# Starting every SBUF tile of a TensorE-bound kernel at a multiple of 128 bytes

## The chip, the cores and the metric

The kernel runs on one core of one Trainium2 chip. The metric is the device time of one execution in microseconds (us). The names of the engines are those of the profile: PE is TensorE's matmul, PEld its weight load, DVE VectorE, ACT ScalarE, POOL GpSimd, SP SyncE, whose queue issues the transfers.

## What is computed

Three parts follow each other: a recurrent attention over 768 steps (32 heads in 4 batches, head size 48), a dense gated layer, and a dense mixture of eight experts whose gates are normalised eight times over rows and columns. Cut to what matters:

```
state = zeros(B, H, D, D)                         # B, H, S, D = 4, 8, 768, 48
for t in range(S):
    cur = einsum('bhd,bhe->bhde', u * k[t], v[t])
    y[t] = einsum('bhd,bhde->bhe', r[t], state + cur)
    state = w[t][..., None] * state + einsum('bhd,bhe->bhde', k[t], v[t])
x = y as (3072, 384)
x = ((x @ w1) * (x @ w2) @ w3) @ w_out            # inner width 1024
P = exp(x @ w_gate - max), 8 times scaled by its row sums and column sums
out = sum over e in 0..7 of P[:, e] * (relu(x @ w1[e]) @ w2[e])   # 384 -> 1024 -> 384
```

## The kernel before

**Split products.** The matmuls that carry the weight are float32r ones (four bytes an element, in one pass). A float32 operand is split into a high part and a low part, and a product is the sum of three matmuls: high by high, and the two mixed ones. So each such product is three matmuls into one PSUM bank. A few smaller products (`w34ps`, `trn`, `sc`, `yt`, `up`, `pl`) are plain float32 ones.

**Attention and dense part** (up to some 440 us). The attention goes in 24 units of 128 steps. Its steps are written out by hand in the table `START` and then in slices of the main loop; the dense layer's matmuls `pa`, `pb` (inputs by `w1h`, `w1l`, `w2h`, `w2l`) and `po` (`w34h`, `w34l` by `gh`, `gl`) fill the same order, 576 of each, every one with 384 moving columns. The product of the third and the output weights, `w34ps`, is made at the start by plain float32 matmuls of 384 columns.

**Experts** (the rest). `phase(n)`, n from 0 to 63, is one pair of weight blocks (k = n // 4) with one quarter of the tokens (sb = n % 4). The first layer is a matrix product with 15 instead of 18 block products: each of the 15 products is six matmuls `zp`, of 256 columns, with the stationary operand from `w1c` and the moving one from `xc`. VectorE and ScalarE put the products together in `ct` and split the result in `hh` (high) and `hl` (low). The second layer runs one phase behind: matmuls `yp` with `hh` or `hl` stationary and the weights `w2h`, `w2l` moving, 384 columns. Between two products of `zp` stand three, six or nine `yp`; the order of the program decides, since all of it is written in order and nothing is scheduled at run time. The weights of block i lie in the tiles `w1c` number i % 3 and `w2h`/`w2l` number i % 4; phases of block pair k use the first-layer weights 2k and 2k+1.

**Where tiles lie.** Tile pools are stacked from the left of a partition's SBUF (const, moe, mw, att, later m2) or from its right (tmp, later wp, m1, xp). Every tile takes its size in bytes a partition, rounded up to 32. A few tiles of odd size (`d1`, `lowb`, `nat_w`, `Ft`, `Gt`, `T12`, `cc`, and in the experts' part `mx`, `nmx`, `rs`, `cs`) shift all that follow them on their side, and the right side's upper end is not at a multiple of 128 either. In the built program, the tiles that matmuls of the heavy kind read start here (bytes in a partition, and the rest on division by 128):

```
tile                          before: start, rest      after: start, rest
w1h, w1l, w2h, w2l (dense)    89440.., 96              89600.., 0
w34h, w34l, gh, gl, xhl       20320.., 96              20480.., 0
xc0, xc1, xc2, xc3            149472.., 96             149376.., 0
w1c number 0 and 1            145376.., 96             145280.., 0
w1c number 2                  71456.., 32              71936.., 0
w2h, w2l number 0 and 1       126944.., 96             126848.., 0
w2h, w2l number 2 and 3       55072.., 32              55552.., 0
hh, hl                        22304.., 32              22784.., 0
wo, w3c (plain float32)       44896.., 96              45056.., 0
```

Inside these tiles a matmul's operand starts a multiple of 512 bytes on, so that the rest of the tile's start is also that of the operand. A stationary operand is 512 bytes of each partition, a moving one 1024 (`zp`) or 1536 bytes.

Of the kernel before, what the change touches and what calls it, by code (L numbers as in the profile page):

```python
# [11 lines left out]
F32 = mybir.dt.float32  # L12
F32R = mybir.dt.float32r
BF16 = mybir.dt.bfloat16
# [47 lines left out]
def tile_rwkv_moe_sinkhorn_moe(  # L62
# [19 lines left out]
    B, H, S, D = SHAPE  # L82
    NT, DM = out.shape
    P = 128
    FF = moe_w3.shape[0] * P
    E = e_w2.shape[0] * 2 * P // FF
    DP = 64
    NP = H // 2
# [7 lines left out]
    NTT = NT // P  # L96
# [19 lines left out]
    const = ctx.enter_context(tc.tile_pool(name="const", bufs=1))  # L116
    ident = const.tile([P, P], F32, name="ident")
    mask = const.tile([P, DP], F32, name="mask")
    eye = const.tile([P, DP], F32, name="eye")
    d1 = const.tile([P, 16 * 33 + 1], BF16, name="d1")  # L120
    GP = 32
    gate = const.tile([P, KD, GP], F32, name="gate")
    lowb = const.tile([P, 1], F32, name="lowb")
    nc.vector.memset(lowb, LOW_BIAS)
    lt = const.tile([GP * UB, P], F32, name="lt")
    nc.vector.memset(gate, 0.0)
# [9 lines left out]
    for c in range(2):  # L136
        nc.scalar.activation(eye[64 * c:64 * c + 64, :], ident[64 * c:64 * c + 64, 64 * c:64 * c + 64], AF.Copy)
        nc.gpsimd.affine_select(out=mask[64 * c:64 * c + 64, :], in_=mask[64 * c:64 * c + 64, :],
                                compare_op=ALU.is_gt, fill=0.0, base=0, pattern=[[1, DP]],
                                channel_multiplier=-1)  # L140

    st_moe = ExitStack()
    moe = st_moe.enter_context(tc.tile_pool(name="moe", bufs=1))
# [3 lines left out]
    att = st_attn.enter_context(tc.tile_pool(name="att", bufs=1))  # L147
# [8 lines left out]
    SRC = {"r": (rt, NP * P), "k": (kt, NP * P), "v": (v, H * DP), "w": (w, 16 * 33 + 1),  # L156
           "rn": (rn, H * D), "kn": (kn, H * D)}
    nat = {}
    for nm in SRC:
        for j in range(2):  # L160
            nat[nm, j] = att.tile([P, SRC[nm][1]], F32, name=f"nat_{nm}{j}")

    def load(u_, nms):
        for nm in nms:
# [96 lines left out]
    st = defaultdict(dict)  # L261
# [7 lines left out]
    def tot(n):  # L269
        return st[n]["F"].rearrange("p (b s) -> p b s", s=33).rearrange("p (c b) s -> p b c s", b=2)  # L270
# [4 lines left out]
        nc.gpsimd.tensor_tensor(t, t, ub, op=ALU.mult)  # L275

    def scan_f(n):
        st[n]["F"] = t = att.tile([P, 528], F32, tag="F", name="Ft")
        nc.vector.tensor_tensor_scan(t, nat["w", n % 2][:, 0:528], d1[:, 0:528], 0.0, op0=ALU.mult, op1=ALU.add)

    def scan_g(n):
        st[n]["G"] = t = att.tile([P, 529], F32, tag="G", name="Gt")
        nc.vector.tensor_tensor_scan(t[:, 2:529][:, ::-1], nat["w", n % 2][:, 2:529][:, ::-1],
                                     d1[:, 2:529][:, ::-1], 0.0, op0=ALU.mult, op1=ALU.add)

    def small(n):
        d, tv = st[n], tot(n)[:, :, :, 32]
        d["M"] = att.tile([P, 2, 8], F32, tag="M", bufs=2, name="Mt")
        d["T12"] = att.tile([P, NP, 2], F32, tag="T12", bufs=2, name="T12")
        nc.vector.reciprocal(d["M"], tv)  # L290
        nc.vector.tensor_tensor(d["T12"].rearrange("p a b -> p (a b)"), tv[:, 0, :], tv[:, 1, :], op=ALU.mult)

# [20 lines left out]
                                    op=ALU.mult)  # L313

    def cc(n):
        st[n]["cc"] = t = att.tile([P, H], F32, tag="cc", bufs=2, name="cc")
        nc.vector.tensor_reduce(t, st[n]["rk"], axis=AX.X, op=ALU.add)

    def ec(n):
# [104 lines left out]
    def stage_a0(n):  # L424
        rk(n)
        aux.extend([lambda f=f: f(n) for f in (scan_f, scan_g, small, ks, rp, kx, rx)] + [lambda: (cc(n), ec(n))])
# [345 lines left out]
    def ld_u():  # L772
        nc.sync.dma_start(ub.rearrange("p h d -> p (h d)"), u.rearrange("h d -> (h d)").partition_broadcast(P))

    STEP = dict(ld=ld, lw=lw, ex=ex_, jn=jn, hi=hi, lo=lo, w34=w34, ws=ws, w34l=w34l_, ldu=ld_u, rk=rk, scanF=scan_f, scanG=scan_g,
                small=small, ks=ks, rp=rp, kx=kx, rx=rx, cc=cc, ec=ec, sc=sc, trn=trn, kn=kn_, cp=cp_, yt1=yt1, up=up_,
                Sn=sn_, yt2=yt2, xraw=xraw, xd=xd_, xh=x_high, xl=x_low, pa=pa, asb=asb, pb=pb, gs=gs, gh=gh_, gl=gl_,
                po=moe_x2, L=lambda nm, n: load(n, (nm,)))
# [5 lines left out]
    for s in range(S0, NSL):  # L784
        n, ph = s // 4, s % 4
# [60 lines left out]
    so = {}  # L846

    def open2():
        st_ps.close()
        st_moe.close()  # L850
        m2 = pools["m2"] = ctx.enter_context(tc.tile_pool(name="m2", bufs=1, reuse_waits="tile"))
        pools["y"] = ctx.enter_context(tc.tile_pool(name="ps2", bufs=1, space=PSUM, reuse_waits="tile"))
        for nm, sh in (("ones", [P, P]), ("Pm", [P, NTT, E]), ("mx", [P, 1]), ("nmx", [P, 1]), ("mrow", [1, P]),
                       ("rs", [P, NTT]), ("cs", [P, E])):
            so[nm] = m2.tile(sh, F32, name=nm)
        nc.vector.memset(so["ones"], 1.0)

    hb = {}
# [64 lines left out]
    def phase(n):  # L923
# [8 lines left out]
        def after(r):  # L932
            if ORDER.index(r) % 4 == 3 or r == ORDER[-1]:
                release(n, GOF[r])
            while at["slot"] in due:
                for f in due.pop(at["slot"]):
                    f()
            at["slot"] += 1
            if ex:
                ex.popleft()()  # L940
            if sk and at["sk"] and ORDER.index(r) in SKP:
                sk.popleft()()
            if n == 0:
                i_ = ORDER.index(r)
                if i_ < PO:
                    moe_x2(NB - 1, i_, PO)
                if i_ == PO - 1:
                    open2()
                if i_ == 11:
                    y_fill(0)  # L950
                y_units((0, 0, 2, 2, 4)[max(0, i_ - 10)])
            elif n == 1:
                y_units(YN1[r])
            else:
                y_units(YN[r])
# [283 lines left out]
```

## Time and profile before

| what | value |
|---|---|
| three timed runs, us | 1945.58, 1946.57, 1946.62 |
| median, us | 1946.57 |
| profiled execution, us | 1946.4, from first to last instruction; no other time of it is shown |
| granted TensorE clock | 1.000 of full speed in every stretch shown |
| busy: PE, PEld | 1919.9 us (99%), 1872.1 us (96%) |
| busy: DVE, ACT, POOL | 1381.8 us (71%), 686.2 us (35%), 647.2 us (33%) |

Busy time of matmuls comes from modelled ends and overlaps: a matmul of 337 ns can follow the one before after half that time. What one matmul costs in a row of them is the step from one to the next, which the chain of work that ended last shows as a piece's length over its count.

### The profile page before, as it was taken

How to read it: one execution, taken by the hardware profiler on the slowest of the kernel's cores; microseconds unless marked ns; L12 is line 12 of the kernel's file. 1: busy time of each engine (PE TensorE's matmuls, PEld its weight loads, DVE VectorE, ACT ScalarE, POOL GpSimd, SP SyncE). 2: the span in 40 equal slices, each digit the busy share in tenths (PEclk: the TensorE clock that was granted, in tenths of full speed). 3: DMA queues.
4: the chain of work that ended last, by engine and by line, in shares of the span. 5: the costliest groups of instructions: out<-in, count | busy, mean ns of one | idle time of the engine just before them, and what ended most of it. 6: DMA issues, size and time to landing. Idle time of an engine off the chain costs nothing.

```text
span 1946.4 us, 38115 instructions
## 1 busy us (share of the span) xinstructions
PE 1919.9 (99%) x15499; PEld 1872.1 (96%) x15499; DVE 1381.8 (71%) x2409; ACT 686.2 (35%) x1322; POOL 647.2 (33%) x867
## 2 busy tenths in 40 slices
PE   6999999999999999999999999999999999999999
PEld 3799999999999999999999999999999999999999
DVE  7865777765887876666767676666676767667666
ACT  6733333344333333233333233333333333333322
POOL 6856666635332312222222222221313231312200
PEclk9999999999999999999999999999999999999999
DMA  9632444347655555454545555555454555555453
GB/s 371 228 95 81 138 132 137 104 151 247 224 177 202 184 190 187 174 213 172 202 177 193 186 193 181 187 185 195 172 202 176 199 188 186 188 179 189 167 202 118
DMA packets 90494, 353.76 MB, mean 182 GB/s; under 512 B 10384, under 2 KB 34256, under 8 KB 64592
## 3 DMA queue, kind: packets, MB, share of 16 engines
q1 hardware_dynamic: 90320, 351.34, 51.4%
q8 instruction: 122, 2.00, 0.4%
q14 instruction: 52, 0.43, 0.1%
HBM read 329.67 MB, written 20.45 MB: 180 GB/s over the span
## 4 chain that ended last, share of the span: by engine, by line
PE 96%; DVE 2%; DMA 1%; ACT 1%; issue 0%; SPq 0%; DVEq 0%; ACTq 0%
PE yp L114 41%; PE zp L114 35%; PE po L114 5%; PE pa L114 5%; PE pb L114 4%; PE w34ps L114 2%; PE yt L114 1%; PE sc L114 1%; PE trn L114 1%; PE up L114 1%; DMA raw<-in_moe_w_out_dram 0%; PE pl L114 0%; DMA raw<-in_moe_w_dram 0%; DVE cvp L229 0%; DMA xraw<-xraw 0%
## 5 line engine op out<-in xcount | busy, mean ns | idle before, releaser
L114 PE MATMUL zp<-xc,w1c 128*128 128x256 f32 x5760 | 815.4, 281 | 1.0 <-DVE ct L894 0.5
L114 PEld LDWEIGHTS zp<-xc,w1c 128*128 128x128 f32 x5760 | 783.6, 189 | 3.8 <-DVE ct L897 1.4
L114 PE MATMUL yp<-w2h,hh 128*128 128x384 f32 x1536 | 516.9, 337 | 0.0
L114 PE MATMUL yp<-w2h,hl 128*128 128x384 f32 x1536 | 516.3, 336 | 0.5 <-DVE hl L891 0.5
L114 PE MATMUL yp<-w2l,hh 128*128 128x384 f32 x1536 | 513.9, 335 | 0.0
L886 ACT ACTIVATE hh<-ct 128x512 fp32r<-128x512 f32 x384 | 237.1, 632 | 538.1 <-DVE ct L894 269.8
L894 DVE TENSOR_TENSOR ct<-ct,zp 128x512 f32<-128x512 f32 x576 | 381.0, 683 | 53.2 <-PE zp L114 47.5
L616 POOL TENSOR_TENSOR w1c<-w1s,w1c 128x512 fp32r<-128x512 f32 (+1 forms) x120 | 127.7, 1064 | 796.4 <-PE yp L114 487.9
L901 ACT ACTIVATE ct<-zp 128x512 f32<-128x512 f32 x256 | 153.3, 599 | 455.9 <-PE zp L114 455.9
L114 PEld LDWEIGHTS yp<-w2h,hh 128*128 128x128 f32 x1536 | 290.9, 189 | 0.2 <-issue 0.2
L114 PEld LDWEIGHTS yp<-w2h,hl 128*128 128x128 f32 x1536 | 288.1, 188 | 1.0 <-DVE hl L891 0.9
L114 PEld LDWEIGHTS yp<-w2l,hh 128*128 128x128 f32 x1536 | 288.3, 188 | 0.0
L1066 DVE SCALAR_TENSOR_TENSOR acc<-yp,Pm,acc 128x384 f32<-128x384 f32 x336 | 205.5, 612 | 109.4 <-PE yp L114 109.2
L891 DVE SCALAR_TENSOR_TENSOR hl<-ct,hh 128x512 fp32r<-128x512 f32 x384 | 273.8, 726 | 0.0
L897 DVE TENSOR_TENSOR ct<-ct,zp 128x512 f32<-128x512 f32 x128 | 88.0, 688 | 168.4 <-PE zp L114 168.4
L897 DVE TENSOR_TENSOR ct<-zp,ct 128x512 f32<-128x512 f32 x128 | 88.3, 690 | 78.2 <-PE zp L114 69.6
L616 POOL TENSOR_TENSOR w1c<-w1raw,w1c 128x128 fp32r<-128x128 f32 (+1 forms) x90 | 55.0, 612 | 205.6 <-ACT w1c L612 205.6
L608 POOL TENSOR_TENSOR w1s<-w1raw 128x128 f32<-128x128 f32 x240 | 121.0, 525 | 0.2
L483 POOL TENSOR_TENSOR gl<-gs,gh 128x384 fp32r<-128x384 f32 x64 | 74.2, 1160 | 109.3 <-ACT gh L479 106.6
L114 PE MATMUL pa<-xhl,w1h 128*128 128x384 f32 x384 | 101.7, 345 | 1.2 <-ACT w34s L255 1.2
L114 PE MATMUL pb<-xhl,w2h 128*128 128x384 f32 x384 | 98.1, 336 | 0.4 <-DVE cv L230 0.4
L474 DVE TENSOR_TENSOR gs<-pb,asb 128x384 f32<-128x384 f32 x64 | 35.4, 553 | 71.5 <-PE pb L114 49.3
(130 smaller groups left out, 1906.2 us busy)
## 6 DMA issues: line engine op xcount, KB each, us to landing
xc<-xd SPq DMA_DIRECT2D x192, 1024.0 KB, 4.8
xc<-xd SPq DMA_DIRECT2D x64, 768.0 KB, 4.3
xd<-x2s SPq DMA_DIRECT2D x53, 256.0 KB, 2.8
w1raw<-in_e_w_dram SPq DMA_DIRECT2D x32, 384.0 KB, 3.1
w2raw<-in_e_w_dram SPq DMA_DIRECT2D x32, 384.0 KB, 3.1
raw<-in_moe_w_dram SPq DMA_DIRECT2D x8, 1024.0 KB, 8.9
nat_w<-in_w_dram SPq DMA_DIRECT2D x24, 264.5 KB, 3.3
nat_k<-in_kt_dram SPq DMA_DIRECT2D x24, 256.0 KB, 4.0
```

The lines of the kernel that those rows point to most:

```text
L114: nc.tensor.matmul(o, lhsT, rhs, start=start, stop=stop, **kw)
L474: nc.vector.tensor_tensor(t, m_t.pop(("pb", blk, f)), m_t.pop(("asb", blk, f)), op=ALU.mult)
L483: nc.gpsimd.tensor_tensor(gl[:, f, :], m_t.pop(("gs", blk, f)), gh[:, f, :].bitcast(F32), op=ALU.subtract)
L608: eng.tensor_tensor(tmp_[:, many.index(r), :], at_(a), at_(b), op=ALU.add if sg == 1 else ALU.subtract)
L616: eng.tensor_tensor(lo[:, d0:d1, :], sv, hi[:, d0:d1, :].bitcast(F32), op=ALU.subtract)
L886: nc.scalar.activation(hh, src, AF.Relu)
L891: nc.vector.scalar_tensor_tensor(hl, src, 0.0, hh.bitcast(F32), op0=ALU.max, op1=ALU.subtract)
L894: nc.vector.tensor_tensor(o, a, b_, op=ALU.add)
L897: nc.vector.tensor_tensor(o, a, b_, op=ALU.subtract)
L901: nc.scalar.activation(t, src, AF.Copy)
L1066: nc.vector.scalar_tensor_tensor(dst, yp, so["Pm"][:, tt, e:e + 1], dst, op0=ALU.mult, op1=ALU.add)
```

## The change

A tile of 96 bytes that nothing reads is put at the right end (`edge`), and the tiles of odd size are allocated with more elements and cut back to the old shape by a slice, so that each operand has the same shape as before. With that nearly every tile begins at a multiple of 128 bytes (the tiles `Mt`, `T12` and `cc` of 64 bytes come in pairs, and the second of a pair begins 64 bytes on). No instruction is added, removed or moved: on each engine the program has the same instructions in the same order with the same waits. The tile `mrow` of m2 now stands ahead of the four small ones.

```diff
-    d1 = const.tile([P, 16 * 33 + 1], BF16, name="d1")
+    d1 = const.tile([P, 16 * 36], BF16, name="d1")[:, 0:16 * 33 + 1]
     GP = 32
     gate = const.tile([P, KD, GP], F32, name="gate")
-    lowb = const.tile([P, 1], F32, name="lowb")
+    lowb = const.tile([P, GP], F32, name="lowb")[:, 0:1]
...
+    edge = ctx.enter_context(tc.tile_pool(name="edge", bufs=1, side="right"))
+    edge.tile([P, 24], F32, name="edge")
...
-            nat[nm, j] = att.tile([P, SRC[nm][1]], F32, name=f"nat_{nm}{j}")
+            nat[nm, j] = att.tile([P, -(-SRC[nm][1] // 32) * 32], F32, name=f"nat_{nm}{j}")[:, 0:SRC[nm][1]]
...
-        st[n]["F"] = t = att.tile([P, 528], F32, tag="F", name="Ft")
+        st[n]["F"] = t = att.tile([P, 544], F32, tag="F", name="Ft")[:, 0:528]
...
-        st[n]["G"] = t = att.tile([P, 529], F32, tag="G", name="Gt")
+        st[n]["G"] = t = att.tile([P, 544], F32, tag="G", name="Gt")[:, 0:529]
...
-        d["T12"] = att.tile([P, NP, 2], F32, tag="T12", bufs=2, name="T12")
+        d["T12"] = att.tile([P, 2 * NP, 2], F32, tag="T12", bufs=2, name="T12")[:, 0:NP, :]
...
-        st[n]["cc"] = t = att.tile([P, H], F32, tag="cc", bufs=2, name="cc")
+        st[n]["cc"] = t = att.tile([P, 2 * H], F32, tag="cc", bufs=2, name="cc")[:, 0:H]
...
-        for nm, sh in (("ones", [P, P]), ("Pm", [P, NTT, E]), ("mx", [P, 1]), ("nmx", [P, 1]), ("mrow", [1, P]),
-                       ("rs", [P, NTT]), ("cs", [P, E])):
+        for nm, sh in (("ones", [P, P]), ("Pm", [P, NTT, E]), ("mrow", [1, P])):
             so[nm] = m2.tile(sh, F32, name=nm)
+        for nm, n_ in (("mx", 1), ("nmx", 1), ("rs", NTT), ("cs", E)):
+            so[nm] = m2.tile([P, 32], F32, name=nm)[:, 0:n_]
```

## Rows read from the trace of the kernel before

**Rows 1.** Cores: span and mean granted TensorE clock.

```profile
core 0: 1946.4 us, clock 1.000
```

**Rows 2.** The page: busy time of each engine, share, instructions.

```profile
PE 1919.9 (99%) x15499; PEld 1872.1 (96%) x15499; DVE 1381.8 (71%) x2409; ACT 686.2 (35%) x1322; POOL 647.2 (33%) x867
```

**Rows 3.** Chain that ended last: shares by engine (page), by line (chain view).

```profile
PE 96%; DVE 2%; DMA 1%; ACT 1%; issue 0%; SPq 0%; DVEq 0%; ACTq 0%
...
by line: PE yp L114 41.0%; PE zp L114 34.8%; PE po L114 5.3%; PE pa L114 4.8%; PE pb L114 4.5%; PE w34ps L114 1.8%; PE yt L114 1.3%; PE sc L114 0.6%; PE trn L114 0.6%; PE up L114 0.5%; DMA raw<-in_moe_w_out_dram 0.5%; issue 0.4%; PE pl L114
```

**Rows 4.** Groups of PE by line and shape: count, busy, mean ns.

```profile
L114 PE MATMUL zp<-xc,w1c 128*128 128x256 f32 x5760 | 815.4, 281 | 1.0 <-DVE ct L894 0.5 <-DVE ct L897 0.5
L114 PE MATMUL yp<-w2h,hh 128*128 128x384 f32 x1536 | 516.9, 337 | 0.0
L114 PE MATMUL w34ps<-wo,w3c 128*128 128x384 f32 x128 | 47.2, 521 | 3.2 <-DVE w3c L230 3.2
```

**Rows 5.** Chain in order of time, early stretch: start us, us, what.

```profile
34.15 0.44 PE trn L114 x4
49.70 8.39 PE w34ps L114 x26
```

**Rows 6.** The same chain: dense part, experts, and the last piece.

```profile
128.12 3.12 PE po L114 x18
1013.51 1.43 PE zp L114 x12
1929.37 13.54 PE yp L114 x78
```

**Rows 7.** Stretches of four phases, k = 6 to 13: busy by engine, clock, DMA.

```profile
1004.06:1097.18 93.12, 93.12 (x649) 93.03 (x649) 64.63 (x103) 30.49 (x58) 23.13 (x38) 1.00 0.53 187
1097.18:1189.50 92.32, 92.32 (x649) 92.23 (x649) 64.32 (x103) 30.22 (x57) 23.11 (x38) 1.00 0.54 188
1189.50:1281.73 92.23, 92.23 (x649) 92.12 (x649) 64.37 (x103) 30.30 (x57) 23.22 (x38) 1.00 0.54 189
1281.73:1374.59 92.86, 92.86 (x650) 92.77 (x649) 64.55 (x103) 30.44 (x58) 23.20 (x38) 1.00 0.53 187
1374.59:1467.41 92.82, 92.82 (x649) 92.74 (x649) 64.41 (x103) 30.36 (x58) 23.16 (x38) 1.00 0.52 188
1467.41:1559.73 92.32, 92.32 (x650) 92.23 (x649) 64.32 (x103) 30.27 (x58) 23.14 (x38) 1.00 0.53 188
1559.73:1652.85 93.12, 93.12 (x650) 93.03 (x649) 64.62 (x103) 30.50 (x58) 23.13 (x38) 1.00 0.53 187
1652.85:1745.17 92.32, 92.32 (x650) 92.23 (x649) 64.32 (x103) 30.23 (x57) 23.11 (x38) 1.00 0.54 188
```

**Rows 8.** Stretches of 20 us after the experts begin: same columns.

```profile
480.00:500.00 20.00, 19.75 (x140) 19.17 (x140) 16.79 (x31) 9.13 (x17) 9.92 (x17) 1.00 0.90 308
580.00:600.00 20.00, 20.00 (x141) 19.90 (x140) 17.93 (x35) 8.23 (x16) 5.65 (x9) 1.00 0.59 211
```

**Rows 9.** Who waited for whom, PE: total us, times, longest.

```profile
PE sc L114 <- POOL Rt L312: 14.0, 1, 14.0
PE w34ps L114 <- DVE w3c L230: 3.2, 2, 2.6
```

**Rows 10.** Who waited for whom, all engines: total us, times, longest.

```profile
ACT ct L901 <- PE zp L114: 455.9, 252, 5.2
DVE ct L897 <- PE zp L114: 237.9, 176, 4.2
DVE acc L1066 <- PE yp L114: 109.2, 102, 1.6
```

**Rows 11.** DMA issues by line: KB each, median us from issue to landing.

```profile
xc<-xd SPq DMA_DIRECT2D x192, 1024.0 KB, 4.8
xc<-xd SPq DMA_DIRECT2D x64, 768.0 KB, 4.3
```

## The prediction

> **What bounds the kernel now.** I read the cores first: one core, 1946.4 us, the granted clock 1.000 throughout, so TensorE stands at 2.4 GHz, the upper of its two levels [rows 1]. The profiled execution lies 0.2 us under the median of the timed runs, 1946.57, so a sum made against it holds for both. Then the engines: PE is busy 99% of the span, the next one, DVE, 71% [rows 2]. Busy PE time is modelled, so the chain that ended last decides: 96% of it is PE, 41.0% `yp` and 34.8% `zp`, the dense `po`, `pa` and `pb` 5.3, 4.8 and 4.5% [rows 3]. In the list of waits PE's longest is 14.0 us, once, and the next 3.2 us [rows 9]; ACT and DVE wait for PE instead [rows 10]. So the time is that of PE working off its list, and what a change does is what it does to the step from one matmul to the next. Everything else is slack unless PE becomes much faster.
>
> **What one matmul costs.** The groups give counts: 5760 `zp`, and three lines of 1536 `yp`, 4608 in all [rows 4]; `pa`, `pb`, `po` are 1728. The reader should take the steps from the chain, not from the mean durations. In plain float32, four `trn` of 128 columns take 0.44 us (110 ns each) and 26 `w34ps` of 384 columns 8.39 us (322.7 ns each) [rows 5]. The slope is 212.7 ns over 256 columns, 0.83 ns a column: two cycles of 2.4 GHz, and what is left over is 322.7 - 320 = 2.7 ns and 110 - 106.7 = 3.3 ns. In float32r, 18 `po` take 3.12 us and 78 `yp` 13.54 us (173.3 and 173.6 ns for 384 columns), 12 `zp` 1.43 us (119.2 ns for 256) [rows 6]. The slope is about 54 ns over 128 columns: one cycle a column. But what is left over is 173.3 - 160 = 13.3 ns and 119.2 - 106.7 = 12.5 ns, four times that of plain float32. 13.3 ns is 32 cycles, and 32 columns of four bytes are 128 bytes.
>
> So a float32r stream of 1536 bytes costs as much as 13 pieces of 128 bytes rather than 12, one of 1024 bytes about as much as 9 rather than 8. That is what a stream costs that starts off such a boundary, if it is fetched by pieces of 128 bytes at one piece in 32 cycles. All these operands start 32 or 96 bytes past a multiple of 128. `w34ps` starts off it too, but it uses a column only every second cycle, so an extra piece would be hidden there.
>
> **Do addresses matter at all?** Eight stretches of four phases each do the same work, 360 `zp` and 288 `yp`, with PE never idle, and differ only in which tiles the weights lie in [rows 7]. Their times are 93.12, 92.32, 92.23, 92.86, 92.82, 92.32, 93.12 and 92.32 us; the first and the seventh are equal, as are the second and the eighth, six stretches apart, which is the period of tiles taken modulo 3 and modulo 4. In the first, fourth and seventh (k = 6, 9, 12) all `zp` weights start at rest 96: mean 93.03 us. In the other five half of them (180) start at rest 32: mean 92.40 us. So 180 weights at 32 instead of 96 save 0.63 us, 3.5 ns each. Between k = 6 and 9 the `w2` tiles go from mostly 96 to mostly 32: 0.26 us less. With rest 32 the first piece holds 96 useful bytes, with 96 only 32. The direction fits the reading by pieces: the more of the first piece is used, the cheaper. Rest 0 lies at the end of that row.
>
> **The change, part by part.** No instruction is added or moved, so the terms are steps times counts.
>
> - *The float32r matmuls.* No row shows one that starts on a boundary. From below: the columns alone, 106.7 and 160 ns. From above: as now. I take the columns and 3 ns, the rest of the plain float32 rows, nearest in kind since they load weights before each matmul too: 109.7 and 163 ns. The mean step now comes from the chain's shares [rows 3]: 34.8% of 1946.4 us is 677 us over 5760 `zp`, 117.6 ns; 41.0% is 798 us over 4608 `yp`, 173.2 ns. `zp`: 7.9 ns x 5760 = 45.5 us. `yp`: 10.2 ns x 4608 = 47.0 us. `pa`, `pb`, `po`: 10.3 ns x 1728 = 17.8 us, of which 95% count, as the three hold 284 us of the chain where 1728 steps of 173.3 ns would be 299: 16.9 us. Sum 109.4 us.
> - *What comes back as waits.* PE's lead shrinks where DVE is densest: 17.93 of 20 us at 580 us, 16.79 of 20 at 480 us [rows 8]. With 7% less PE time the first would be 96% DVE. It lasts a few such slices; over k = 6 to 13 DVE is at 64.4 of 92.6 us [rows 7] and would be at 75%. I give back 3 us in all. Transfers of `xc` land in 4.8 or 4.3 us [rows 11], and in a phase of 23 us each group is asked for as soon as its last reader is done, so they stay hidden.
> - *Other engines' operands, transfers, the order of `mrow`.* Their instructions have the same shapes. Should DVE or ACT gain or lose a few per cent by the new starts, it goes into their waits for PE (455.9 and 237.9 us [rows 10]): nothing.
>
> 1946.4 - 109.4 + 3 = 1840 us. With no rest at all per matmul the gain would be 3 ns x 12096 = 36 us more: 1801 with nothing given back.
>
> On what a step costs, the Trainium skill (TensorE: Matmul & The Clock Gate, Back-to-back issue gap) gives columns over 2.4 GHz plus about 2.5 ns. The plain float32 rows agree with its rest, the float32r rows are five times above it; by the page the sum would be an estimate of 1946.4 - 115 + 3 = 1834 us.
>
> **The rivals.**
>
> - *Same: the 32 cycles belong to every float32r matmul, wherever it starts.* Then `yp` stays at 173.3. For it: the rest is nearly equal at 256 and 384 columns, as a fixed price would be, and `yp` with both operands at 32 costs no less than `po` with both at 96. Against it: plain float32 switches weights as often and pays 3 ns, and the means of [rows 7] would have to come from where the tiles lie and not from their rest. Only those 0.63 us would go: 1940 to 1950 us, for me 1946. On this the Trainium skill (SBUF — State Buffer, the box on cachelines in the section on Door 1) speaks against the change: it has lines of 16 bytes, and every tile of before starts on one already. No row here shows a price for 16 bytes; by that rule the gain is nothing.
> - *Partial: alignment is worth only as much as the step from 96 to 32 was.* 3840 `zp` weights at 3.5 ns (13.4 us), the 5760 moving `xc` (20.2 us) likewise, `w2` tiles at 1 to 2 ns (2 to 5 us), and the dense part's two operands, 0 to 7 ns x 1728 (0 to 12 us): 15 to 50 us, 1896 to 1931. For it: these are the only prices of an address that a row shows. Against it: the remaining 12 ns would need another cause that plain float32 doesn't have.
> - *Slower: equal rests collide.* A weight load reads while the matmul before it streams. With all operands at rest 0 both streams cross their boundaries together, as now in the all-96 stretches, which are the slowest. If equality costs and not the rest 96, the ten stretches that are mixed today rise to the all-96 price, 0.63 us each (6.3 us), and a little with the `yp`: 1953 us. It decides if a four-phase stretch takes more than 92.6 us. Against it: `yp` with moving and stationary both at 32 is equal as well and is cheaper than with 96 and 32.
>
> **How the numbers follow.** Forecast 0.54, partial 0.17, same 0.15, slower 0.14. A difference of 0.2% (3.9 us) is about what a measurement of this kernel can tell from no change, so faster is 0.54 + 0.17 = 0.71, same 0.15, slower 0.14. The likeliest one's own range is 1801 to 1871 us: from no rest at all, to a rest of 5 instead of 3 ns (2 ns x 12096 = 24 us) and 10 us of waits instead of 3. To hold 8 in 10, the whole range must take in partial and nearly all of same; it leaves out the slower case: 1801 to 1948.
>
> **What would show it.** Right: 18 `po` in 2.95 us and 12 `zp` in 1.32 us of the chain; four phases in 86.4 to 87 us, equal for all k since no rest differs any more; PE still some 95% of the chain, with a few new waits of PE for DVE `ct`, `hl` or `acc` near 480 to 600 us; `w34ps` and `trn` as before. Wrong: `yp` at 173 ns (same), stretches that are equal but near 92 us (the rests mattered, the 32 cycles are something else), or stretches above 93 us (collision). If PE falls to 163 ns a `yp` and the time doesn't follow, DVE's dense slices have become the bound.

## The result, and the profile after

The changed kernel is slower: 1958.14 us median of five runs (1957.64 to 1958.44) against 1946.05 us of five runs of the kernel before, ratio 1.006, 95% interval 1.0048 to 1.0072. The profiled execution spans 1956.7 us, 10.3 us more than before.

Where did they come from? The share of the chain that ended last, by line, of the changed kernel:

```profile
by line: PE yp L114 41.1%; PE zp L114 34.9%; PE po L114 5.2%; PE pa L114 4.7%; PE pb L114 4.5%; PE w34ps L114 1.4%; PE yt L114 1.3%; PE sc L114 0.6%; PE trn L114 0.6%; DMA nat_kn<-in_kn_dram 0.5%; PE up L114 0.5%; DMA raw<-in_moe_w_dram 0.4
```

`yp` holds 41.1% of 1956.7 us, 804 us, and `zp` 34.9%, 683 us, against 798 and 677 us in [rows 3]: 6 us more each. The two parts of the program, in the windows view of the changed kernel (as in [rows 7]: the stretch and its length, the busy us and count of instructions of PE, PEld, DVE, ACT and POOL, the granted clock, the busy share of the DMA engines and their GB/s):

```profile
0.00:440.36 440.36, 420.61 (x5022) 376.78 (x5023) 321.22 (x677) 197.28 (x415) 272.08 (x266) 1.00 0.47 159
440.36:1956.70 1516.34, 1511.48 (x10479) 1508.12 (x10478) 1063.22 (x1732) 489.51 (x908) 372.40 (x601) 1.00 0.53 187
```

and of the kernel before, cut where its first `zp` starts:

```profile
0.00:442.02 442.02, 420.64 (x5022) 376.76 (x5022) 320.54 (x677) 197.38 (x415) 272.38 (x266) 1.00 0.47 158
442.02:1946.40 1504.38, 1499.30 (x10479) 1495.29 (x10478) 1061.29 (x1732) 488.80 (x908) 374.81 (x601) 1.00 0.53 189
```

The experts' part takes 12.0 us more, with the same count of matmuls, the same clock and PE idle for some 5 us in either; the part ahead of it 1.7 us less, 1.6 us of which is PE's one long wait, now 12.4 us:

```profile
PE sc L114 <- POOL Rt L315: 12.4, 1, 12.4
```

The dense part already gives the first answer. All its float32r operands stood at rest 96 before and stand at rest 0 now, with equal rests in both kernels, so that only the place where both start changed and not their distance. In the chain, 18 `po` still take the 3.12 us of [rows 6], not the 2.95 us that the prediction named as its sign:

```profile
121.74 3.12 PE po L114 x18
```

The stretches of four phases that answer to [rows 7] (k = 6 to 13), changed kernel:

```profile
1006.74:1100.12 93.38, 93.38 (x649) 93.31 (x649) 64.60 (x103) 30.45 (x58) 23.05 (x38) 1.00 0.53 186
1100.12:1193.99 93.87, 93.87 (x649) 93.83 (x649) 64.75 (x103) 30.46 (x57) 23.01 (x38) 1.00 0.53 185
1193.99:1287.20 93.21, 93.21 (x650) 93.14 (x650) 64.50 (x103) 30.38 (x57) 22.97 (x38) 1.00 0.54 187
1287.20:1380.39 93.19, 93.19 (x649) 93.11 (x649) 64.48 (x103) 30.32 (x57) 23.01 (x38) 1.00 0.53 187
1380.39:1474.03 93.64, 93.64 (x649) 93.59 (x649) 64.66 (x103) 30.46 (x58) 23.01 (x38) 1.00 0.52 186
1474.03:1566.95 92.92, 92.92 (x650) 92.85 (x650) 64.44 (x103) 30.30 (x57) 23.00 (x38) 1.00 0.52 187
1566.95:1660.33 93.38, 93.38 (x649) 93.31 (x649) 64.61 (x103) 30.45 (x58) 23.09 (x38) 1.00 0.52 186
1660.33:1754.20 93.87, 93.87 (x649) 93.83 (x649) 64.75 (x103) 30.47 (x57) 23.01 (x38) 1.00 0.51 185
```

Every one is slower than its fellow in [rows 7], by 0.3 to 1.6 us, mean 93.43 against 92.64 us. There are two more things to see. They still differ from each other, and repeat after six, though every operand now begins at rest 0 modulo 128: so something finer than the rest modulo 128 counts. And the slowest (k = 7, 13) and the fastest (k = 11) all mix left and right tiles, while those with all `zp` weights on the right (k = 6, 9, 12) lie between.

### The profile page after: what moved, and what is told of

It reads as the page before. It is cut to its first block, busy times and chain, and to the rows that moved or that the text cites. A ratio compares the mean times of both kernels' runs of the same rounds, so it can differ in the third digit from the quotient of the medians.

```text
span 1956.7 us, 38115 instructions
## 1 busy us (share of the span) xinstructions
PE 1932.1 (99%) x15499; PEld 1884.9 (96%) x15499; DVE 1384.4 (71%) x2409; ACT 686.8 (35%) x1322; POOL 644.5 (33%) x867
## 4 chain that ended last, share of the span: by engine, by line
PE 95%; DVE 2%; DMA 1%; ACT 1%; issue 0%; SPq 0%; DVEq 0%; ACTq 0%
PE yp L114 41%; PE zp L114 35%; PE po L114 5%; PE pa L114 5%; PE pb L114 4%; PE w34ps L114 1%; PE yt L114 1%; PE sc L114 1%; PE trn L114 1%; DMA nat_kn<-in_kn_dram 1%; PE up L114 1%; DMA raw<-in_moe_w_dram 0%; PE pl L114 0%; DVE Sn L387 0%; DVE cvp L232 0%
```

## The theories, and the experiments

**Boundary theory** (the prediction's): a stream costs a piece of 128 bytes more when it starts off a boundary. **Fixed price**: a float32r matmul costs 32 cycles more than its columns, wherever it starts. **Relative theory**: a weight load reads while the matmul ahead of it streams, and the distance of the two addresses decides what a step costs. What I call distance is the rest of the stationary operand less that of the moving one, modulo 256 bytes (the series below show that modulus). Right tiles (`xc`, `w1c` 0 and 1, `w2` 0 and 1) of before are at 224, left ones (`w1c` 2, `w2` 2 and 3, `hh`, `hl`) at 32; of the change, at 128 and 0. A stationary `w1c` 2 or `hh`, `hl` on the left stood 64 after a moving tile on the right before, and stands 128 after it now.

**m1_steps: one distance at a time, nothing else running.** A new kernel with one row of matmuls after the other:

```diff
+for n, tag in ((384, "y"), (256, "z")):
+    for d in range(0, 512, 32):
+        out.append((tag + "d" + chr(97 + d // 32), "r", n, 0, 8192 + d // 4))
+    for s in (32, 64, 96):
+        out.append((tag + "s" + chr(97 + s // 32), "r", n, s // 4, 8192 + s // 4))
...
+for i in range(rep):
+    m = m0 + 512 * (i % 3)
+    w = w0 + 128 * (i % 5)
+    nc.tensor.matmul(o[:, 0:n], t[:, w:w + P], t[:, m:m + n], start=i == 0, stop=i == rep - 1)
```

> Only series of 36 matmuls each, with nothing to compute and nothing to wait for (the output is filled with a copy of the last bank). In each series the moving operand begins at a fixed place and the stationary one a distance d further on, taken modulo 512 bytes; d goes from 0 to 480 in steps of 32, for 384 and 256 columns of float32r. Boundary theory (the start modulo 128 counts): with d = 0 both operands begin at a multiple of 128 and the step is near 163 and 110 ns, with both moved by 32, 64 or 96 bytes it is 173 and 119. Fixed-price theory: 173.3 and 120 ns in every series. Relative theory (the weight load reads while the matmul before it streams, and the distance of the two decides): 173.3 and 120 ns at d = 0 however both are moved, and other values at other distances, near 116 ns for 256 columns at a distance like 192 or 320.

Rows picked from the chain in order of time (start us, us, what). In the names, y is 384, z 256 and x 512 columns, p plain float32 with 384; d and a letter give the distance (a 0, b 32, c 64 and so on), s and a letter by how much both operands are moved (b 32, c 64):

```profile
23.98 6.24 PE yda L60 x36
36.47 6.28 PE ydc L60 x36
49.11 6.33 PE yde L60 x36
55.45 6.36 PE ydf L60 x36
68.05 6.36 PE ydh L60 x36
74.41 6.26 PE ydi L60 x36
124.85 6.27 PE ysb L60 x36
131.12 6.27 PE ysc L60 x36
187.34 4.31 PE zda L60 x36
195.91 4.24 PE zdc L60 x36
200.15 4.23 PE zdd L60 x36
204.38 4.27 PE zde L60 x36
221.46 4.31 PE zdi L60 x36
255.56 4.32 PE zsb L60 x36
298.49 8.19 PE xda L60 x36
306.68 8.40 PE xdc L60 x36
339.87 23.22 PE pda L60 x72
```

At distance 0 and on a boundary (`yda`, `zda`, `xda`) a step is 173.3, 119.7 and 227.5 ns for 384, 256 and 512 columns: the columns and 13 to 14 ns, whatever the length. Both operands off the boundary by 32 or 64 (`ysb`, `ysc`, `zsb`) cost the same within 1 ns. That ends the boundary theory: there was no piece to save. The distance does count: 384 columns take 173.3 ns at 0, 174.4 at 64 (`ydc`), 175.8 at 128 (`yde`) and 176.7 at 160 and 224 (`ydf`, `ydh`); 256 columns 117.8 at 64 (`zdc`) and 118.6 at 128 (`zde`). 512 columns pay 5.8 ns for 64 (`xdc`). At 256 (`ydi`, `zdi`) it is as at 0. So before the change `yp` with `w2` on the right paid 1.1 ns for its 64 and pays 2.5 for its 128, and `zp` with `w1c` 2 loses 0.8 ns of the 1.9 that it had over distance 0. Over 2304 such `yp` and 1800 such `zp` that is 4.7 us: the right sign, but less than half of the 12.0 us.

**off32_all: the change, off the boundary, all distances kept.**

```diff
+    const.tile([P, 8], F32, name="low")
     ident = const.tile([P, P], F32, name="ident")
...
-    edge.tile([P, 24], F32, name="edge")
+    edge.tile([P, 16], F32, name="edge")
```

> The changed kernel with everything moved 32 bytes up, the left side by a filler of 32 bytes at the start of the first pool, the right side by a smaller edge: every operand begins at rest 32 modulo 128, all distances between operands stay those of the changed kernel. Boundary theory: as fast as before or faster, 1935 to 1946 us. Relative theory: as the changed kernel, 1958 us, the same times of the stretches of four phases within 0.1 us.

It takes 1958.99 us, ratio to before 1.0069 (1.0052 to 1.0086), and its stretches k = 6 to 8 are those of the change to 0.02 us:

```profile
1006.74:1100.13 93.39, 93.39 (x650) 93.32 (x650) 64.63 (x103) 30.47 (x58) 23.12 (x38) 1.00 0.53 186
1100.13:1194.00 93.87, 93.87 (x650) 93.83 (x650) 64.75 (x103) 30.46 (x57) 23.02 (x38) 1.00 0.53 185
1194.00:1287.19 93.19, 93.19 (x649) 93.12 (x649) 64.47 (x103) 30.38 (x57) 22.98 (x38) 1.00 0.53 187
```

So in the experts' part, too, it is not the rest modulo 128.

**same512: the change, aligned as before it, with all distances 0.**

```diff
+        m2.tile([P, 32], F32, name="gap")
```

> The changed kernel with 128 bytes of filler at the start of the pool m2, so that every operand of the experts' matmuls begins at rest 384 modulo 512, on both sides; all begin at multiples of 128 as in the change. Boundary theory: no difference from the changed kernel, 1958 us. Relative theory: every matmul pays exactly 32 cycles; a stretch of four phases takes 84.48 us + 648 x 13.33 ns = 93.12 us, the same for every k, against 92.9 to 93.9 in the changed kernel: 1954 us.

1949.06 us, ratio 1.0014 (1.0005 to 1.0023): 9 of the 12 us are back, by 128 bytes of filler that change no alignment. All stretches are now equal:

```profile
1002.72:1095.52 92.80, 92.80 (x649) 92.71 (x649) 64.44 (x103) 30.34 (x58) 23.07 (x38) 1.00 0.54 188
1095.52:1188.32 92.80, 92.80 (x649) 92.72 (x649) 64.44 (x103) 30.33 (x58) 23.07 (x38) 1.00 0.53 188
```

They are 0.3 us below the 93.12 expected from single steps, and the total is 5 us below the 1954 us worked out from that: a step depends a little on what stands ahead of it, too.

**edge_only, left_only: one half of the change each.** The first adds the filler at the right end to the kernel before, the second leaves it out of the change.

```diff
     (edge_only, against the kernel before)
+    edge = ctx.enter_context(tc.tile_pool(name="edge", bufs=1, side="right"))
+    edge.tile([P, 24], F32, name="edge")
...
     (left_only, against the change)
-    edge = ctx.enter_context(tc.tile_pool(name="edge", bufs=1, side="right"))
-    edge.tile([P, 24], F32, name="edge")
```

> One half of the change: the kernel before with only the filler at the right end. Right operands at rest 128 modulo 256, left ones at 32, so left stationary operands stand 160 after right moving ones. By the steps of the series at 160 (176.8 ns for 384 columns, 119.8 for 256) the experts take 10 us more than before, 4 us more than in the changed kernel: 1956 us, up to 1966 if the price doubles as it did for the whole change. Boundary theory: the right side is aligned, so no slower than the kernel before, 1946 us.

> The other half: odd sizes rounded up, no filler at the right end. Right operands at rest 224 modulo 256, left ones at 0: distance 32, at which the series take 173.3 ns (384 columns) and 118.3 (256). Relative theory: within 3 us of before, 1943 to 1948 us. Boundary theory: half of the operands aligned, between before and the change: 1950 us or so.

1957.36 us, ratio 1.0054 (1.0039 to 1.0069), and 1955.76 us, ratio 1.0046 (1.0032 to 1.006). Each half alone costs nearly what the whole does. The second expectation missed: I had summed steps of rows with one distance throughout, and 32 is cheap in such rows. It isn't where rows of `zp` and `yp` with different distances take turns, as the next run shows.

**m2_loops: the experts' pattern alone.** Six matmuls of 256 and six of 384 columns, with operands at the rests of each kernel and each mix of tiles, and nothing else running:

```diff
+sides("be", 224, 32)       # before: right, left
+sides("af", 128, 0)        # the change
+sides("ed", 128, 32)
+sides("le", 224, 0)
+for s in range(0, 256, 32):
+    out.append(("xs" + chr(97 + s // 32), (256 - s) % 256, 0, 0, 0, 0))
```

> Only the experts' pattern of six matmuls of 256 columns and six of 384, six times over for each layout, with nothing to wait for (the output is filled with a copy of the last bank). Each layout gives the rests modulo 256 of xc, of the two w1c, of w2 and of hh, hl. Relative theory: the layouts of before and of the changed kernel give the loop times that those kernels have (before: 1740 to 1767 ns a loop, all rests equal: 1760 at most), so nothing but PE's own reads is needed; best are layouts with xc 64 to 96 or 192 to 224 bytes below the rest and the others equal, some 20 ns a loop less than all equal. Rival, traffic of other engines or transfers on the same banks: without that traffic all layouts give the same loop.

Rows picked from PE's in order of time (start us, us; a loop is the step from one row to the next of the same name). In the names, be is before and af the change, with a last letter a where `w1c` and `w2` lie on the right and d where the first `w1c` and `w2` lie on the left; xs has all rests equal, but `xc` lower by 0 (a), 32 (b), 64 (c) and so on:

```profile
32.76 0.88 PE L57 MATMUL zbea<-data 128*128 128x256 f32 x6
34.53 0.88 PE L57 MATMUL zbea<-data 128*128 128x256 f32 x6
62.57 0.86 PE L57 MATMUL zbed<-data 128*128 128x256 f32 x6
64.31 0.86 PE L57 MATMUL zbed<-data 128*128 128x256 f32 x6
97.58 0.89 PE L57 MATMUL zafa<-data 128*128 128x256 f32 x6
99.36 0.89 PE L57 MATMUL zafa<-data 128*128 128x256 f32 x6
125.87 0.89 PE L57 MATMUL zafd<-data 128*128 128x256 f32 x6
127.66 0.89 PE L57 MATMUL zafd<-data 128*128 128x256 f32 x6
283.13 0.87 PE L57 MATMUL zxsa<-data 128*128 128x256 f32 x6
284.88 0.28 PE L57 MATMUL zxsa<-data 128*128 128x256 f32 x1
304.30 0.84 PE L57 MATMUL zxsc<-data 128*128 128x256 f32 x6
306.03 0.84 PE L57 MATMUL zxsc<-data 128*128 128x256 f32 x6
```

Before: 1.77 and 1.74 us; the change: 1.78 and 1.79 us; all equal: 1.75 us; `xc` 64 lower: 1.73 us. So PE's own reads are enough; no other engine and no transfer is needed. Layout d, among the best of before, is the worst of the change: that is the spread over k seen above. In mean over the six mixes and the later loops of each, before takes 1750 ns, left_only 1764, edge_only 1769, the change 1770, and the profiled spans stand in the same order: 1946.4, 1954.2, 1955.6, 1956.7 us. Of the layouts that were expected to be best only the one with `xc` 64 lower is: 96 and 192 lower take the 1753 ns of all equal, 224 lower 1767.

**xc96 and xc64: tiles placed by distance.** The kernel before, with the left side brought to the right side's rest by a filler, and `xc` 96 or 64 bytes lower than the rest (64: a tile that grows by 256 bytes keeps its rest modulo 256, and a start 192 bytes into it is then 64 bytes lower):

```diff
     (xc64; xc96 has 40 for 48 and 24 for 16)
+        nx = 2 * len(XP_[g][4]) * T
+        if g < 2:
+            t = pools["w"].tile([P, nx + 64], F32R, tag=f"xc{g}", name=f"xc{g}")[:, 48:48 + nx]
+            t = t.rearrange("p (a b c) -> p a b c", a=2, c=T)
...
     ld_x(0, 3)
+    pools["m"].tile([P, 16], F32, name="gap")
...
+        m2.tile([P, 48], F32, name="gap")
```

> Placed by the table of the series, not by 128: the kernel before with 192 bytes of filler in front of m2, so that left and right operands have the same rest modulo 256, and with xc alone 96 bytes lower. Every weight load then stands 96 after a moving xc (117.3 ns for 256 columns) and 0 after a moving w2 (173.3 ns). Relative theory: 12.7 us less than before by the series' steps, 1934 us (1930 to 1940); stretches of four phases equal for all k, some 92.0 us. Boundary theory: nothing is aligned more than before, 1946 us.

> As the run with xc 96 bytes lower, but 64 bytes lower. The loops of the experts' pattern by themselves took 1753 ns with all rests equal, 1753 with xc 96 lower and 1727 with xc 64 lower; the run with 96 lower took what the one with equal rests took, as those loops say. If the distances of concurrently read operands are all there is, the real kernel gains 26 ns for each 12 matmuls of the experts against equal rests (1949 us): 10368 / 12 x 26 ns = 23 us, 1926 us (1922 to 1935), a stretch of four phases near 91.4 us. If something else than PE's reads decides in the full kernel, it stays near 1946.

96 lower: 1948.97 us, ratio 1.0012 (1.0003 to 1.002), as with all equal; the sum of single steps missed by 15 us, while the loops, which had 1753 ns for both, had it right. 64 lower: 1923.67 us, ratio 0.9885 (0.9869 to 0.9902). Its stretches take 91.1 to 91.2 us, and a loop of six and six, 1011.05 to 1012.78, the 1.73 us that it took alone:

```profile
994.64:1085.84 91.20, 91.20 (x649) 91.13 (x649) 64.20 (x103) 30.27 (x57) 23.17 (x38) 1.00 0.54 191
```

```profile
1011.05 0.84 PE L114 MATMUL zp<-xc,w1c 128*128 128x256 f32 x6
1011.73 0.34 PE L114 MATMUL yp<-w2h,hh 128*128 128x384 f32 x1
...
1012.78 0.84 PE L114 MATMUL zp<-xc,w1c 128*128 128x256 f32 x6
```

Six `zp` now take 0.68 us, 113.3 ns each: half of the 32 cycles is gone. The six `yp` take the other 1.05 us, 175 ns each, no less than before.

**m3_map: all layouts at steps of 32 bytes**, the loops of m2_loops for each of 512 layouts.

> The same loops without the rest of the kernel (the output is filled with a copy of the last bank), four for each of 512 layouts: w1c at rest 0, and xc, w2 and hh, hl at all multiples of 32 below 256. Relative theory: the loop with xc 64 lower, 1727 ns, is among the fastest; none comes near the 1600 ns of the columns alone, as every matmul keeps most of its 32 cycles; alignment of all four to 128 bytes gives no better loops than other rests do. Boundary theory: the eight layouts with all four at 0 or 128 are the fastest.

Loops go from 1720 to 1787 ns, median 1760; the eight layouts with all rests at 0 or 128 have a mean of 1768, worse than the median. One of the two fastest (`xc` and `w2` at 192, the stationary `w1c`, `hh`, `hl` at 0), and one of the slowest (`xc` and `w1c` at 0, the others at 192):

```profile
3066.41 0.85 PE L40 MATMUL zggga<-data 128*128 128x256 f32 x6
3068.13 0.85 PE L40 MATMUL zggga<-data 128*128 128x256 f32 x6
```

```profile
408.60 0.88 PE L40 MATMUL zgagg<-data 128*128 128x256 f32 x6
410.38 0.88 PE L40 MATMUL zgagg<-data 128*128 128x256 f32 x6
```

**moving64: the map's fastest layout in the kernel.** As xc64, and `w2h`, `w2l` 64 bytes lower too:

```diff
-    pools["m"].tile([P, 16], F32, name="gap")
...
+        f0, f1 = (48 if k == 2 else 0), (16 if k in (1, 3) else 0)
+        hi = pool.tile([P, f0 + 2 * DM], F32R, tag=f"w2h{k}", name=f"w2h{k}")[:, f0:]
+        lo = pool.tile([P, 2 * DM + f1], F32R, tag=f"w2l{k}", name=f"w2l{k}")[:, 0:2 * DM]
+        hi, lo = (x.rearrange("p (i d) -> p i d", i=2) for x in (hi, lo))
```

> From the map of 512 layouts: w1c and hh, hl at one rest, and both moving operands, xc and w2, 64 bytes lower: 1720 ns a loop of 12 matmuls, the fastest of the map, against 1727 with xc alone lower. Relative theory: 10368 / 12 x 7 ns = 6 us less than the run with xc alone 64 lower (1923.7 us): 1918 us, 1914 to 1923. If the map's small differences don't carry over to loops of other lengths than 6 and 6, 1921 to 1930.

1919.12 us, ratio 0.9856 (0.984 to 0.9872): 27 us less than before and 39 less than the change, with every stretch at 90.8 us:

```profile
993.58:1084.38 90.80, 90.80 (x650) 90.68 (x650) 64.15 (x104) 30.26 (x57) 23.22 (x38) 1.00 0.55 192
1084.38:1175.17 90.79, 90.79 (x649) 90.67 (x649) 64.13 (x104) 30.25 (x57) 23.22 (x38) 1.00 0.55 192
```

## Why the prediction was wrong

- *What bounds the kernel.* Right. PE holds 95% of the chain after, its waits hardly moved, and all that changed came from the step between matmuls.
- *"That is what a stream costs that starts off such a boundary, if it is fetched by pieces of 128 bytes at one piece in 32 cycles."* This is the step that failed, and with it the whole term of 109.4 us. The 13.3 ns were there, but they stay with a start on the boundary: 18 `po` take 3.12 us at rest 96 and at rest 0. In m1_steps and off32_all, too, the start makes no difference, and the rest is 13 to 14 ns for 256, 384 and 512 columns alike. The text itself named the fixed price as a rival and had its best evidence in hand, an equal rest at two lengths; I weighed the plain float32 rows against it. They do pay less (72 entries of 384 columns in 23.22 us, 322.5 ns each; the series has 36 matmuls, so that the profile holds each as two entries), but that they hide an extra piece was argued, not shown. That rival's time, 1946 us, missed as well: the price is fixed as to the boundary, not as to the distance.
- *"Rest 0 lies at the end of that row."* Failed too. [rows 7] did show that addresses count, by 0.63 us a stretch; but moving `w1c` from 96 to 32 changed its distance to `xc` from 0 to 64 as well, and I took the rest for the cause. One series over two positions can't tell the two apart.
- *What comes back as waits, other engines, transfers.* Nothing showed up, as said; DVE's 64.4 us a stretch became 64.6. Where PE gained 27 us (moving64) PE stayed the bound.
- *Rivals.* The side was that of the slower one, and its place fits the runs: the addresses of a weight load and of a streaming matmul. Its condition was wrong: equal rests do not collide most (same512, 92.80 us in every stretch, below all eight of the change, of which 92.92 is the nearest); the distance of 128 that the change makes between left and right costs more (loops of 1770 against 1753 ns). So its price was too small as well, 6.3 us against the 12.0 us of the experts' part. On the same side as the fixed-price rival, the Trainium skill's lines of 16 bytes (SBUF — State Buffer, section on Door 1) fit off32_all and the series with both operands moved; they say nothing of distances.
- *The Trainium skill's gap of columns and 2.5 ns* (TensorE: Matmul & The Clock Gate, Back-to-back issue gap) was not reached by any float32r row shown here; the lowest, 113.3 ns for 256 columns, is 6.6 ns above the columns. The section gives it for an isolated matmul and sets it apart from a stream of weight loads and matmuls, which these rows are.

## What to carry to other kernels

When PE bounds a kernel with float32r matmuls and never waits, put its steps between matmuls beside the columns over the clock, and compare stretches of equal work whose tiles differ: if they differ, where the tiles lie is a knob. Turn it by measuring the real pattern alone for many layouts, not by a round number: here the same left and right stacks cost +0.6% at multiples of 128 bytes and -1.4% with the moving operands 64 bytes below the stationary ones. Before an overhead is put down to a cause, see whether it scales as that cause would, and vary the cause alone.

## What had not been expected of the hardware

- A float32r matmul with its weight load takes 13 to 14 ns (some 32 cycles at 2.4 GHz) more than its columns at distance 0, at 256, 384 and 512 columns alike. At best half of it went (113.3 ns for 256 columns). What it is stays open, and so does why a plain float32 entry of 384 columns takes only 2.5 ns more than two cycles a column (322.5 ns).
- The distance of the weights' address to that of the moving operand changes the step by up to 3.4 ns of 173 (384 columns), 2.2 ns of 120 (256 columns) and 5.8 ns of 228 (512 columns), with a period of 256 bytes over the distances tried (0 to 480 bytes). Distance 0 is among the cheapest for 384 and 512 columns and among the dearest for 256. That the load collides with the matmul ahead, and not with its own, is argued, not shown: in most rows here the two have the same distance.
- Steps have a memory: single distances, summed, gave 1934 us for xc96, which took 1949, while loops of the real pattern, run alone, put all the kernels in the right order. By those loops the change would have cost 864 x 20 ns, some 18 us, where the experts' part lost 12.0; the kernel's other loops, with three or nine `yp` or with twelve `zp`, weren't run alone.
- Each profile begins its experts' part at a slightly other time (439.3 us in same512, 442.0 before); why the change's one long wait ahead of them is shorter (1.6 of the 1.7 us) was not followed further.
